# One ring of single PSUM banks, rounding scratch in PSUM, later block stores and a re-dealt set of sums, in a retention block followed by a SwiGLU feed-forward

## The chip, the cores and the metric

The kernel runs on one core of a Trainium2 chip. The metric is the device time of one execution in microseconds (us). The profile is that of one execution, taken by the hardware profiler. Its engine names are PE (TensorE, the matmuls; PEld is its weight load), DVE (VectorE), ACT (ScalarE), POOL (GpSimd) and SP (SyncE, which here only issues transfers). Lines such as L653 are lines of the kernel before.

## The reference

The weight matrices are fp64 arrays, the rest fp32. First a retention layer, then a normalised gated feed-forward on its output:

```python
# q, k, v: (8 batches, 8 heads, 576 positions, 64)
scores = scale * np.matmul(q, k.transpose(0, 1, 3, 2))
gamma = 1.0 - 2.0 ** (-5.0 - np.arange(H))
Dmat = np.where(rel >= 0, gamma ** rel, 0.0)      # rel = i - j
attn = np.matmul(scores * Dmat, v)
# (B,H,S,D) -> x: (4608 tokens, 512)
xn = x / np.sqrt(np.mean(x * x, -1) + 1e-6) * rms_g
g = xn @ w_gate                                    # 512 -> 1536
out = (g / (1 + np.exp(-g)) * (xn @ w_val)) @ w_out   # 1536 -> 512
```

The weight matrices are read as pairs of 32-bit words, a low and a high one.

## The kernel before

**Units.** The 4608 tokens are nine units of 512 (`u` 0 to 8). Attention for one batch and two heads is a *slot* (`j`, 32 of them): `scores`, `states`, `weigh`, `sums`, `values`, `carried`. A unit's feed-forward has two halves: *up* (gate and value, with the gating, into `h`) and *across* (`h` times `w_out`). Units 0 and 1 use plain matmuls for up (`up_plain`); units 2 to 8 use a scheme of seven products in place of eight for each 2 x 2 split (`up`), and every across uses that scheme twice, so seven products `xzwyxzw`, each made of seven smaller ones.

**Rounding.** While units 0 and 1 go up, the fp64 weights are turned to fp32 by integer work. There are 36 *halves* (512 KB loads, four scratch places `spare`, half `i` in place `i % 4`). A half takes three steps of the generator `rounding`: `exponent` (L862, VectorE, followed by two ScalarE instructions), `mantissa` (L877, L880, L884) and `join` (L901). The exponents lie in the last third of the scratch place. After every fourth half GpSimd makes the sums of the seven-product scheme (L912) and SP stores the block to DRAM: two transfers for an up block (`finish_set`, L922), seven for an out block (`finish_slice`, L928). Only then is the load of half `i + 4` issued (L849). Blocks come in the order up 0, 1, 2, out 0, up 3, out 1, up 4, 5, out 2. The loop over `up_plain` counts its 48 groups of matmuls in `now`; each group is one bank, four matmuls of 128 x 512, and then up to three rounding steps (`weights(3)`), so one half. Attention slots, the transposes of q and k (`prepare`) and their transfers (`fetch`) are hung on certain values of `now`.

**Across.** For every one of the seven products, four sums of quarters of its operand are needed (`inner_sums`, L694, four instructions of 128 x 384). They lie in one of two places of `inner`. In units 2 to 8 GpSimd makes all but four of the early ones (the list at L697 names units 0 and 1 only); sums 0 and 1 before the first product, sum `n + 2` after product `n`. The first half of a product (`late=False`) does without the sums. ScalarE keeps x, VectorE adds y, z and w to the kept values (`add`, L749). In the middle of it VectorE also normalises the next unit's x: `root_2`, then `norm_2` with four scalings (L514) and four sums of x (L524), all at step 6 of across.

**PSUM.** Eight banks. Three are one tile `trio` (scores and states of a slot; x and half of y in across); five rotate under one tag.

**Order.** The order of instructions on each engine is written by hand: the generators are driven by the loops in `start` and at the end, and each engine takes its instructions in that order. SP issues transfers in that order too.

Of the kernel before, what the change touches and what calls it, by code (L numbers as in the profile page):

```python
# [14 lines left out]
P = 128  # L15
# [26 lines left out]
def kernel(  # L42
# [234 lines left out]
    def scores(j):  # L277

        d = st[j]
        s = d["s"] = trio.tile([P, 3, 512], F32, tag="s", name=f"s_{j}")  # L280
        for c in range(NC + 1):
            i, odd = divmod(c, 2)
            c = min(c, NC - 1)
            for e in range(2):
                nc.tensor.matmul(
                    s[side(odd), e, i * L : i * L + L], lhsT=d["kT"][side(e), c * L : c * L + L],
                    rhs=d["qT"][side(e), c * L : c * L + L], start=True, stop=True,
                )

    def state_of(d, c):  # L290

        i, odd = divmod(c, 2)
        if odd and SC + i * L == 512:
            return d["last"][:, :L]
        return d["s"][:, 1, SC + i * L : SC + i * L + L] if odd else d["s"][:, 2, i * L : i * L + L]

    def states(j):

# [11 lines left out]
    def weigh(j):  # L310

        d = st[j]
        hp = jobs[j][1]
        s = d["s"]
        n = NFULL + 1
        ret = d["ret"] = att.tile([P, 2, n, L], F32, tag="ret", name=f"ret_{j}", bufs=1)
        for e in range(2):
            nc.vector.scalar_tensor_tensor(
                out=ret[:, e], in0=s[:, e, : n * L].rearrange("p (c k) -> p c k", k=L),
                scalar=float(_gamma(H)[2 * hp + e] ** -L),  # L320
                in1=causal.unsqueeze(1).to_broadcast([P, n, L]), op0=ALU.mult, op1=ALU.mult,
            )
# [177 lines left out]
        t_of[u] = y  # L500

    def norm_2(u):

        x = x_of[u]
# [6 lines left out]
        for c in range(NHP):  # L513
            nc.vector.scalar_tensor_tensor(  # L514
                out=x[:, c], in0=x[:, c], scalar=g[:, c : c + 1], in1=rb,
                op0=ALU.mult, op1=ALU.mult,
            )
        if u < 2:
            return
# [158 lines left out]
        return {A11: b11, S1: t1, S3: b12, S2: b11, A12: b21, S4: b22, A22: t1}  # L678

    def inner_of(u, n):  # L680
        return [inner[:, (7 * u + n) % 2, i] for i in range(4)]

    def inner_sums(u, n):

        x = operands_of(u)[ORDER[n]]
        x11, x12 = x[:, :NK, :P], x[:, :NK, P:]
        x21, x22 = x[:, NK:, :P], x[:, NK:, P:]
        i1, i3, i2, i4 = inner_of(u, n)
        eng = nc.vector if 7 * u + n in (4, 7, 10, 12) else nc.gpsimd
        for o, a, b, op in (  # L690
            (i1, x12, x11, ALU.subtract), (i3, x22, x12, ALU.subtract),
            (i2, i3, x11, ALU.add), (i4, x21, i2, ALU.subtract),
        ):
            eng.tensor_tensor(out=o, in0=a, in1=b, op=op)  # L694

    def across(u):
# [4 lines left out]
        b21, b22 = hh[:, NH:, :HU], hh[:, NH:, HU:]  # L701
        t1 = t1_of(u)
        operands = operands_of(u)
        tri = []
        vector = {}
        first = set()

        def banks_of(nm):

            if not tri:  # L710
                tri.append(trio.tile([P, 3, 512], F32, tag="s", name=f"s_out_{u}"))
            t = tri[0]
            if nm == "x":
                return t[:, 0], t[:, 1]
            if nm == "y":
                return t[:, 2], bank(f"yo_{u}")
            return bank(f"{nm}o_{u}"), bank(f"{nm}p_{u}")

        def product(n, nm, w, late):
# [30 lines left out]

        last = u == NU - 1
        if u > 1:
            inner_sums(u, 0)
            inner_sums(u, 1)
        yield
        for n, nm in enumerate("xzwyxzw"):
            w = piece("out", u, n)
            product(n, nm, w, False)
            yield
            product(n, nm, w, True)  # L760
            used()
            if n == 0:
                keep(3, "x")
                nc.vector.tensor_tensor(out=b11, in0=b12, in1=b11, op=ALU.add)
            elif n == 1:
                nc.vector.tensor_tensor(out=t1, in0=b21, in1=b11, op=ALU.subtract)
            elif n == 3:
                add(1, 3, "y")
                add(3, 1, "z")
                add(3, 3, "w")  # L770
                if last:
                    combine(3)
            elif n == 4:
                keep(0, "x")
                if last:
                    combine(0)
            elif n == 5:
                add(2, 1, "z")
                if last:
                    combine(2)  # L780
            elif n == 6:
                add(1, 1, "w")
                if last:
                    combine(1)
            if n + 2 < 7 or u == 0:
                inner_sums(u + (n + 2) // 7, (n + 2) % 7)
            yield
        if not last:
# [41 lines left out]
    def words_of(i):  # L830
        return spare[i % 4][:, :WORDS].bitcast(U32)

    def exp_of(i):
        return spare[i % 4][:, WORDS:]

    def load_half(i, queue):
        if i >= len(halves):
# [20 lines left out]

    def exponent(i):

        w, e = words_of(i), exp_of(i).bitcast(U32)
        nc.vector.tensor_scalar(  # L862
            out=e, in0=w[:, 1::2], scalar1=20, scalar2=0x7FF,
            op0=ALU.logical_shift_right, op1=ALU.bitwise_and,
        )
        f = exp_of(i)
        acts.extend((i, x) for x in (
            dict(out=f, in_=e, bias=most, scale=-1.0),
            dict(out=e, in_=f, bias=top, scale=-(2.0**23)),
        ))  # L870

    def mantissa(i):
# [7 lines left out]
        nc.vector.tensor_scalar(  # L880
            out=hi, in0=hi, scalar1=0xFFFFF, scalar2=0x100000,
            op0=ALU.bitwise_and, op1=ALU.bitwise_or,
        )
        nc.vector.scalar_tensor_tensor(  # L884
            out=lo.bitcast(F32), in0=lo, scalar=2.0**-32, in1=hi, op0=ALU.mult, op1=ALU.add
        )

    def join(i):
# [25 lines left out]
    def finish_set(k):  # L914
# [6 lines left out]
        for o, t in ((w_up_d[k][:, : 3 * BLOCK], w[:, :3]), (w_up_d[k][:, 3 * BLOCK :], s)):  # L921
            nc.sync.dma_start(out=o, in_=t.rearrange("p b c f -> p (b c f)"))  # L922

    def finish_slice(k):
        combine_blocks([slices[:, i, :4] for i in range(7)], S1)
        combine_blocks([slices[:, :, i] for i in range(7)], S1)
        for o in ORDER:
            nc.sync.dma_start(out=w_out_d[o][:, :, k], in_=slices[:, o])  # L928

    n_joined = 0  # L930
    due = False
    sets_used = [0] * 2 * NG
# [7 lines left out]
    def rounding():  # L940
# [4 lines left out]
        for i in range(len(halves)):  # L945
# [31 lines left out]

    def start():

        tables = list(zip((causal, gv, gc, gq, gx), (_causal_table(), *_decay_tables(H, D))))  # L980

        def table(i, queue):
# [51 lines left out]
            act(1)  # L1034
        gather(*squares.pop())
        fetch(FIRST)

        now = 0
        for u, k in (
            (0, 0), (1, 0), (0, 1), (1, 1), (0, 2), (1, 2), (0, 3), (1, 3), (0, 4), (0, 5), (1, 4),  # L1040
# [3 lines left out]
            for i, _ in enumerate(up_plain(u, k)):  # L1044
# [10 lines left out]
                    prepare(FIRST + (now - 10) // 6)  # L1055
                elif now in (12, 18):
                    fetch(FIRST + 1 + (now - 12) // 6)
                elif now == 36:
                    slot(FIRST, rest=False)
                elif now in (40, 42, 44):  # L1060
                    slot(FIRST + (now - 38) // 2)
                elif now in (41, 43, 45):
                    prepare(FIRST + (now - 37) // 2)
                    fetch(FIRST + (now - 35) // 2)
                elif now == 46:
# [25 lines left out]
        for i, _ in enumerate(across(1)):  # L1091
# [5 lines left out]
                root_2(2)  # L1097
            elif i == 8:
                norm_2(2)

    with tc.manual_schedule():
        start()
        for u in range(2, NU):
# [53 lines left out]
```

## Time and profile before

Two timed runs: 1238.75 and 1232.72 us, median 1235.74. The profiled execution spans 1230.5 us.

| stage of the profile | from, us | what it is |
|---|---|---|
| slots 0 to 7 | 0 | attention of batches 0 and 1, first halves rounded |
| up of units 0 and 1, rounding | 58 | 48 groups, slots 8 to 11 towards the end |
| across of units 0 and 1 | 305 | 14 products |
| units 2 to 6 | 376 | each up, four slots, across; about 125 us each |
| units 7 and 8 | about 1005 | up and across without slots |
| last sums and stores | 1224 | end |

Busy over the whole span: PE 1124.3 us, DVE 827.9, POOL 445.1, ACT 249.0. The profile's page also cuts the span in 40 equal slices of 30.8 us and gives each engine's busy share in tenths; `PEclk` is the granted TensorE clock in the same way. In a group line "x16 | 19.5, 1216" is the count, the busy time in us and the mean in ns; in a timeline line the first number is the start, the second the time, and the bracket the idle time before it and what ended it. Transfers move 249.22 MB, 203 GB/s in the mean.

### The profile page before, as it was taken

Reading aid. Unit: us, or ns where it says so; the run is one execution under the profiler, and the core shown is the slowest. Engines: PE = TensorE matmul, PEld = TensorE weight load, DVE = VectorE, ACT = ScalarE, POOL = GpSimd, SP = SyncE. Lnnn points to the kernel's source line nnn. Section 1 sums busy time; section 2 is a strip of 40 time slices with the busy share of each in tenths; the row PEclk is TensorE's granted clock in tenths of the full one; section 3 lists DMA queues with packets and bytes.
Section 4 is the critical chain, followed back from the end, with each engine's and each line's share of the span. In section 5 each row is a group of like instructions: output and inputs, shape, how many; then the busy total and the mean of one; then the engine's idle time right before and its main releaser. Section 6 shows DMA issues by size and latency. Waiting matters only on the chain. (4 is left out here: it accounts for less than half of the span.)

```text
span 1230.5 us, 24167 instructions
## 1 busy us (share of the span) xinstructions
PE 1124.3 (91%) x10086; PEld 925.9 (75%) x10086; DVE 827.9 (67%) x1398; ACT 249.0 (20%) x501; POOL 445.1 (36%) x356
## 2 busy tenths in 40 slices
PE   8889574898999998999899989999999999989997
PEld 6634231355989887988798888888888888879897
DVE  5899675857796779376937793779376834592555
ACT  5433132221111220112012201221122101201110
POOL 0033433342783018400850076006700670184036
PEclk9999887999999999999999999999999999999999
DMA  8566686538977885579557874787666546356361
GB/s 209 149 183 229 157 221 181 212 100 200 350 269 273 230 231 206 183 174 248 198 214 183 215 280 169 199 211 256 233 147 207 192 180 240 138 210 214 122 251 37
DMA packets 255421, 249.22 MB, mean 203 GB/s; under 512 B 193104, under 2 KB 232656, under 8 KB 241104
## 3 DMA queue, kind: packets, MB, share of 16 engines
q1 hardware_dynamic: 253456, 246.59, 64.4%
q8 instruction: 79, 1.29, 0.4%
q10 hardware_dynamic: 1856, 1.09, 0.3%
q14 instruction: 30, 0.25, 0.1%
HBM read 217.55 MB, written 30.08 MB: 201 GB/s over the span
## 5 line engine op out<-in xcount | busy, mean ns | idle before, releaser
L694 POOL TENSOR_TENSOR vi<-h 128x384 f32<-128x384 f32 x78 | 106.2, 1377 | 482.4 <-DVE h L605 459.9
L647 PE MATMUL up<-x,ring 128*128 128x512 f32 x384 | 180.7, 628 | 46.1 <-DVE ring L653 20.6
L647 PEld LDWEIGHTS up<-x,ring 128*128 128x128 f32 x384 | 75.4, 201 | 145.3 <-issue 83.7
L586 PE MATMUL x<-x,ring 128*128 128x256 f32 x672 | 161.4, 383 | 0.0
L586 PE MATMUL w<-sums,ring 128*128 128x256 f32 x672 | 158.7, 379 | 0.0
L586 PE MATMUL z<-x,ring 128*128 128x256 f32 x672 | 158.7, 379 | 0.0
L586 PEld LDWEIGHTS z<-x,ring 128*128 128x128 f32 x672 | 127.7, 190 | 19.9 <-issue 2.9
L586 PEld LDWEIGHTS w<-sums,ring 128*128 128x128 f32 x672 | 127.7, 190 | 17.4
L586 PEld LDWEIGHTS x<-x,ring 128*128 128x128 f32 x672 | 125.1, 190 | 17.4
L800 POOL TENSOR_TENSOR vi<-vi 128x512 f32<-128x512 f32 (+1 forms) x56 | 67.1, 1210 | 42.5 <-DVE vi L749 40.0
L586 PE MATMUL y<-sums,ring 128*128 128x256 f32 x336 | 79.6, 379 | 1.7 <-issue 1.7
L586 PEld LDWEIGHTS y<-sums,ring 128*128 128x128 f32 x336 | 63.8, 190 | 10.7 <-issue 2.1
L731 PE MATMUL s_out<-ring,vi 128*128 128x128 f32 x540 | 67.5, 278 | 2.8 <-POOL vi L694 2.8
L593 DVE TENSOR_TENSOR h<-u,w 128x512 f32<-128x512 f32 x42 | 28.9, 687 | 60.9 <-PE w L586 44.0
L745 ACT COPY vi<-s_out 128x512 f32<-128x512 f32 (+1 forms) x36 | 17.4, 535 | 250.0 <-PE s_out L731 224.7
L731 PEld LDWEIGHTS s_out<-ring,vi 128*128 128x128 f32 x540 | 64.1, 194 | 4.4 <-POOL vi L694 3.9
L912 POOL TENSOR_TENSOR ring<-ring 128x512 f32<-128x512 f32 x24 | 34.5, 1436 | 86.5 <-DVE ring L901 85.6
L612 ACT COPY m<-x 128x512 f32<-128x512 f32 x42 | 24.6, 585 | 189.4 <-PE x L586 189.4
L593 DVE TENSOR_TENSOR u<-m,y 128x512 f32<-128x512 f32 x42 | 28.8, 685 | 50.0 <-PE y L586 47.9
L731 PE MATMUL s_out<-ring,h 128*128 128x128 f32 x384 | 51.8, 292 | 11.3 <-DVE vi L749 11.3
L731 PEld LDWEIGHTS s_out<-ring,h 128*128 128x128 f32 x384 | 49.4, 206 | 13.7 <-DVE vi L749 12.8
L334 DVE SCALAR_TENSOR_TENSOR sum<-sum,gc,s 128x64 f32<-128x64 f32 x192 | 53.9, 281 | 6.8
(214 smaller groups left out, 1930.1 us busy)
## 6 DMA issues: line engine op xcount, KB each, us to landing
ring<-w_out_blocks SPq DMA_DIRECT2D x63, 1344.0 KB, 6.6
ring<-w_up_blocks SPq DMA_DIRECT2D x42, 1792.0 KB, 7.6
w_out_blocks<-vi SPq DMA_DIRECT2D x21, 448.0 KB, 5.7
out_dram<-vi SPq DMA_DIRECT2D x64, 128.0 KB, 3.0
qraw<-in_q_dram SPq DMA_DIRECT2D x96, 72.0 KB, 5.3
kraw<-in_k_dram SPq DMA_DIRECT2D x96, 72.0 KB, 3.2
k<-in_k_dram SPq DMA_DIRECT2D x48, 128.0 KB, 2.9
v<-in_v_dram SPq DMA_DIRECT2D x48, 128.0 KB, 2.8
```

What stands on the lines that cost most here:

```text
L334: nc.vector.scalar_tensor_tensor(out=t[:, c], in0=t[:, c - 1], scalar=gc[:, hp : hp + 1], in1=part, op0=ALU.mult, op1=ALU.add,)
L586: nc.tensor.matmul(ps[:, i * HU : i * HU + HU], lhsT=w[:, PLACE[blk], c, i * P : i * P + P], rhs=t_of[u][blk][:, c], start=(start and i == ...
L593: nc.vector.tensor_tensor(out=o, in0=a, in1=pairs_of(ps), op=ALU.add)
L612: nc.scalar.copy(out=s1, in_=pairs_of(x_))
L647: nc.tensor.matmul(ps, lhsT=w[:, PLACE[blk], c % 2, i * P : i * P + P], rhs=x_of[u][:, c], start=(c == 0), stop=(c == NHP - 1),)
L694: eng.tensor_tensor(out=o, in0=a, in1=b, op=op)
L731: nc.tensor.matmul(ps, lhsT=lhs[:, c], rhs=w[:, s, c], start=((nm, s // 4) not in first), stop=False, skip_group_check=True,)
L745: nc.scalar.copy(out=o, in_=ps)
L800: eng.tensor_tensor(out=t[:, :, o], in0=t[:, :, x], in1=t[:, :, y], op=ALU.add)
L912: nc.gpsimd.tensor_tensor(out=t[o], in0=t[x], in1=t[y], op=op)
```

## The change

It has five parts.

1. **Single banks.** `trio` goes; all eight banks rotate under one tag. A slot's scores and states are three tiles, and each of x, y, z, w in across takes two.
2. **Rounding in PSUM.** From the up stage on, a half's exponents lie in a bank `exp_i`, and L880 writes its masked high words to a bank `man_i` in place of the scratch place. So each of the five VectorE instructions has at most one operand in SBUF that it reads. In groups 0 to 3 one rounding step follows a group instead of three.
3. **Stores behind loads.** `finish_set` and `finish_slice` put their stores on a list; they are issued two halves (up) or four halves (out) after the block's last join, ahead of that half's load. The last out block's stores go after the up pieces of unit 0.
4. **Sums of across, units 2 to 8.** Sum 1 goes to VectorE, ahead of the `b11` addition; sum 2 gets a third place, in `sums_x`; three sums are made before the first product, 3, 4, 5, 6 after products 0, 1, 3, 4.
5. **Norm spread out.** The scalings of the next x come one each at steps 3 to 6 of across, the sums of x at step 8, behind the additions. Slots and transposes in the up stage move by a group or two (the first slot from 36 to 34).

```diff
-    trio = ctx.enter_context(tc.tile_pool(name="trio", bufs=1, space=PS))
-    banks = ctx.enter_context(tc.tile_pool(name="banks", bufs=5, space=PS))
+    banks = ctx.enter_context(tc.tile_pool(name="banks", bufs=8, space=PS))
...
-        s = d["s"] = trio.tile([P, 3, 512], F32, tag="s", name=f"s_{j}")
+        s = d["s"] = [bank(f"s_{j}_{i}") for i in range(3)]
...
     def inner_of(u, n):
-        return [inner[:, (7 * u + n) % 2, i] for i in range(4)]
+        if u > 1 and n == 2:
+            t = sums_x.rearrange("p i c t -> p (i c t)")
+            return list(t.rearrange("p (i c t) -> i p c t", i=4, c=NK))
+        at = (0, 1, None, 0, 1, 0, 1)[n] if u > 1 else (7 * u + n) % 2
+        return [inner[:, at, i] for i in range(4)]
...
-        eng = nc.vector if 7 * u + n in (4, 7, 10, 12) else nc.gpsimd
+        eng = nc.vector if (n == 1 if u > 1 else 7 * u + n in (4, 7, 10, 12)) else nc.gpsimd
...
         if u > 1:
-            inner_sums(u, 0)
-            inner_sums(u, 1)
+            for n in range(3):
+                inner_sums(u, n)
...
-            if n + 2 < 7 or u == 0:
+            if u > 1:
+                if n in (0, 1, 3, 4):
+                    inner_sums(u, {0: 3, 1: 4, 3: 5, 4: 6}[n])
+            elif n + 2 < 7 or u == 0:
...
+        exps[i] = bank(f"exp_{i}") if in_psum else spare[i % 4][:, WORDS:]
...
+        m = bank(f"man_{i}").bitcast(U32) if in_psum else hi
         nc.vector.tensor_scalar(
-            out=hi, in0=hi, scalar1=0xFFFFF, scalar2=0x100000,
+            out=m, in0=hi, scalar1=0xFFFFF, scalar2=0x100000,
...
-            out=lo.bitcast(F32), in0=lo, scalar=2.0**-32, in1=hi, op0=ALU.mult, op1=ALU.add
+            out=lo.bitcast(F32), in0=lo, scalar=2.0**-32, in1=m, op0=ALU.mult, op1=ALU.add
...
+        stores.append((n_joined + 3, [
+            (o, t.rearrange("p b c f -> p (b c f)"))
...
+        stores.append((n_joined + 5, [(w_out_d[o][:, :, k], slices[:, o]) for o in ORDER]))
...
             join(i)
+            n_joined += 1
+            store_blocks(n_joined)
             load_half(i + 4, nc.sync)
-            n_joined += 1
...
-                elif now == 36:
+                elif now == 34:
                     slot(FIRST, rest=False)
...
-                weights(3)
+                weights(3 if now > 3 else 1)
...
             if (u, k) == (0, 5):
                 weights_to(len(halves))
+                store_blocks(len(halves) + 9)
                 refill(1)
...
                 if i == 2:
                     root_2(u + 1)
-                elif i == 6:
-                    norm_2(u + 1)
+                elif i in (3, 4, 5, 6):
+                    scale_x(u + 1, (i - 3,))
+                elif i == 8:
+                    sums_of_x(u + 1)
```

More of the change, by code (lines that the diff above doesn't have):

```diff
@@ L285, in scores @@
                 nc.tensor.matmul(
-                    s[side(odd), e, i * L : i * L + L], lhsT=d["kT"][side(e), c * L : c * L + L],
+                    s[e][side(odd), i * L : i * L + L], lhsT=d["kT"][side(e), c * L : c * L + L],
                     rhs=d["qT"][side(e), c * L : c * L + L], start=True, stop=True,
@@ L294, in state_of @@
             return d["last"][:, :L]
-        return d["s"][:, 1, SC + i * L : SC + i * L + L] if odd else d["s"][:, 2, i * L : i * L + L]
+        return d["s"][1][:, SC + i * L : SC + i * L + L] if odd else d["s"][2][:, i * L : i * L + L]
     def states(j):
@@ L318, in weigh @@
             nc.vector.scalar_tensor_tensor(
-                out=ret[:, e], in0=s[:, e, : n * L].rearrange("p (c k) -> p c k", k=L),
+                out=ret[:, e], in0=s[e][:, : n * L].rearrange("p (c k) -> p c k", k=L),
                 scalar=float(_gamma(H)[2 * hp + e] ** -L),
@@ L502, in norm_2, with scale_x @@
     def norm_2(u):
+        scale_x(u, range(NHP))
+    def scale_x(u, chunks):
         x = x_of[u]
@@ L512, in norm_2 @@
             nc.tensor.matmul(rb, lhsT=ones, rhs=t_of[u], start=True, stop=True)
-        for c in range(NHP):
+        for c in chunks:
             nc.vector.scalar_tensor_tensor(
@@ L517, in norm_2, with sums_of_x @@
             )
-        if u < 2:
-            return
+    def sums_of_x(u):
+        x = x_of[u]
         b11, b12 = x[:, :2, :HU], x[:, :2, HU:]
@@ L703, in across @@
         operands = operands_of(u)
-        tri = []
         vector = {}
@@ L708, in banks_of @@
         def banks_of(nm):
[L710 to L716, printed above, removed]
             return bank(f"{nm}o_{u}"), bank(f"{nm}p_{u}")
@@ L831, in words_of @@
         return spare[i % 4][:, :WORDS].bitcast(U32)
+    exps = {}
     def exp_of(i):
-        return spare[i % 4][:, WORDS:]
+        return exps[i]
     def load_half(i, queue):
@@ L920, in finish_set @@
         )
-        for o, t in ((w_up_d[k][:, : 3 * BLOCK], w[:, :3]), (w_up_d[k][:, 3 * BLOCK :], s)):
-            nc.sync.dma_start(out=o, in_=t.rearrange("p b c f -> p (b c f)"))
+        stores.append((n_joined + 3, [
+            (o, t.rearrange("p b c f -> p (b c f)"))
+            for o, t in ((w_up_d[k][:, : 3 * BLOCK], w[:, :3]), (w_up_d[k][:, 3 * BLOCK :], s))
+        ]))
     def finish_slice(k):
@@ L926, in finish_slice, with store_blocks @@
         combine_blocks([slices[:, :, i] for i in range(7)], S1)
-        for o in ORDER:
-            nc.sync.dma_start(out=w_out_d[o][:, :, k], in_=slices[:, o])
+        stores.append((n_joined + 5, [(w_out_d[o][:, :, k], slices[:, o]) for o in ORDER]))
+    def store_blocks(n):
+        while stores and stores[0][0] <= n:
+            for o, t in stores.pop(0)[1]:
+                nc.sync.dma_start(out=o, in_=t)
+    stores = []
+    in_psum = False
     n_joined = 0
@@ L978, in start @@
     def start():
+        nonlocal in_psum
         tables = list(zip((causal, gv, gc, gq, gx), (_causal_table(), *_decay_tables(H, D))))
@@ L1036, in start @@
         fetch(FIRST)
+        in_psum = True
         now = 0
@@ L1057, in start @@
                     fetch(FIRST + 1 + (now - 12) // 6)
-                elif now == 36:
+                elif now == 34:
                     slot(FIRST, rest=False)
[L1060 to L1065, printed above, removed]
+                elif now in (40, 42, 45):
+                    slot(FIRST + {40: 1, 42: 2, 45: 3}[now])
+                elif now in (41, 44, 46):
+                    n = {41: 2, 44: 3, 46: 4}[now]
+                    prepare(FIRST + n)
+                    fetch(FIRST + n + 1)
+                elif now == 47:
                     close(FIRST + NHP - 1)
-                weights(3)
+                weights(3 if now > 3 else 1)
                 act(2)
@@ L1099, in start @@
                 norm_2(2)
+                sums_of_x(2)
     with tc.manual_schedule():
```

## The prediction

> **What bounds the kernel now.** I read the page first: share of each engine, then the slices.
>
> ```profile
> PE 1124.3 (91%) x10086; PEld 925.9 (75%) x10086; DVE 827.9 (67%) x1398; ACT 249.0 (20%) x501; POOL 445.1 (36%) x356
> ...
> PE   8889574898999998999899989999999999989997
> POOL 0033433342783018400850076006700670184036
> PEclk9999887999999999999999999999999999999999
> ```
>
> TensorE is the bound nearly everywhere, so only its gaps can be won: the dip in slices 5 to 9 (a slice is 30.8 us), and one lighter slice every fourth, where POOL peaks. The clock row drops in the same places. The chain of waits covers only the last 8 us (VectorE's closing sums), so I went on with PE's own waits and then with the timeline of each engine around them.
>
> **Gap 1, weight rounding (58 to 252 us).** Groups of up_plain (one bank, eight records each; 48 of them, numbered by `now`) run at 7.11/2 = 3.56 us when nothing waits: the first line below is groups 4 to 18 without a gap. Then PE, POOL, SP and VectorE at the longest hole:
>
> ```profile
> 82.33 53.24 PE L647 MATMUL up<-x,ring 128*128 128x512 f32 x120 [3.81 <-DVE x L514]
> 157.42 12.04 PE L647 MATMUL up<-x,ring 128*128 128x512 f32 x24 [16.40 <-DVE ring L653]
> 127.03 14.08 POOL L912 TENSOR_TENSOR vi<-vi 128x512 f32<-128x512 f32 x7 [6.20 <-DVE vi L901]
> 141.13 8.47 SPq L928 DMA_DIRECT2D w_out_blocks<-vi  x7
> 149.66 1.52 SPq L849 DMA_DIRECT2D sums<-in_moe_w_val_dram  x1
> 156.34 0.43 DVE L862 TENSOR_SCALAR sums<-sums 128x512 uint32<-128x512 uint32 x1 [13.50 <-DMA sums<-in_moe_w_val_dram]
> ```
>
> SP issues in order: the stores of out block 0 wait for POOL's sums (until 141.1), the next load stands behind them, VectorE starves 13.5 us, PE 16.4. Out block 1 does the same at 198 to 210 (VectorE 11.8, PE 8.8). The groups of VectorE by shape show the second cost:
>
> ```profile
> L884 DVE SCALAR_TENSOR_TENSOR ring<-ring 128x512 f32<-128x512 uint32 x16 | 19.5, 1216 | 0.6
> L884 DVE SCALAR_TENSOR_TENSOR t<-t 128x512 f32<-128x512 uint32 x8 | 5.6, 694 | 0.3
> L880 DVE TENSOR_SCALAR ring<-ring 128x512 uint32<-128x512 uint32 x16 | 17.0, 1063 | 0.6
> L880 DVE TENSOR_SCALAR t<-t 128x512 uint32<-128x512 uint32 x8 | 3.4, 428 | 0.3
> L653 DVE TENSOR_TENSOR ring<-ring,up 128x512 f32<-128x512 f32 x10 | 6.8, 678 | 0.0
> ```
>
> The same instruction takes 694 ns (on t), or on average 1216 (on ring): single ones are 0.69 or 1.64 us, the latter while POOL runs; L653, with one operand in PSUM, keeps 678 beside POOL.
>
> **Gap 2, across.** A product of seven (42 pairs of records) takes 4.69 us, so an across could take 32.8. Unit 2's runs from 462.9 to about 503.9, 41.0 us; units 3 to 6 the same, unit 7 39.4, unit 8 33.9. PE in unit 2, then VectorE:
>
> ```profile
> 471.94 0.94 PE L731 MATMUL zp<-ring,vi 128*128 128x128 f32 x6 [0.83 <-POOL vi L694]
> 488.18 3.85 PE L731 MATMUL s_out<-ring,h 128*128 128x128 f32 x18 [1.61 <-DVE vi L749]
> 476.23 5.69 DVE L514 SCALAR_TENSOR_TENSOR x<-x,rms_k,sq 128x512 f32<-128x512 f32 x4
> 487.45 0.67 DVE L749 TENSOR_TENSOR vi<-vi,s_out 128x512 f32<-128x512 f32 x1
> ```
>
> POOL's sums are late: it makes four instructions for each of the seven, only two sums ahead, and they take 1.32 to 1.44 us, 1.00 when VectorE is quiet. VectorE's norm ops take 1.42 instead of 0.69 in turn, so its y addition starts at 487.45; and the fifth product (x again) waits for that addition only because x and y share the three-bank tile. The wait costs 1.6 us and a slow clock (18 records in 3.85, not 2.17).
>
> **What the Trainium skill says.** "SBUF — State Buffer", section "Who interferes with whom": VectorE and GpSimd share a port pair as an exclusive lock; a VectorE instruction with two SBUF inputs, or in a two-port mode, contends with GpSimd, one with a single SBUF input outside those modes does not. The rows above agree (678 always; 694 against 1640). "VectorE: DVE Perf Modes", section "Why PSUM operands drop a tier", and Mode 2×_2P: the doubled fp32 rate of a one-source op needs SBUF on both sides. So L862 and L880 (420 to 430 ns) lose it when they write PSUM; no row here shows one, so I bound it: below by 430, above by 750; I take 680, the one-rate L653. "TensorE: Matmul & The Clock Gate", section "What's actually happening": an idle window of some 3.4 us halves the clock; the 5.90 us that one group takes after the gap at 192 us agrees.
>
> **The change, part by part.**
>
> *Rounding in PSUM.* Start-to-start, undisturbed, a half costs VectorE now 0.34+0.72+0.46+0.73+0.61 = 2.86 us (L862, 877, 880, 884, 901). With exp and man in PSUM the two one-source ops rise to about 0.60 and 0.72, L877 no longer has to finish first (0.60): 3.26. That is +0.4 x 32 halves = 13 us, against what the lock costs now: L884 16 x 0.52, L877 16 x 0.51 + 9 x 0.27, L880 16 x 0.63, L901 10 x 0.35, L862 3: 36 us. Net VectorE gain 23.
>
> *Stores behind loads.* Stores of an up block go two halves after its last, of an out block four later (14.4 us at 3.6, POOL needs 13.9). The starving of 13.5 and 11.8 goes, but not wholly: when out stores are issued they hold SP 8.5 us and the next load lands about 15 us after (141.1 to 156.3), while VectorE needs it two steps later, 7.2 us: a stall of 7.5, twice. A transfer of q and k (9.5 us of SP, 123.8 to 133.2) stands right before out block 0's stores: another 4; the one before it: 2. Together 21 us (none to 40).
>
> *Sum of groups 4 to 35.* VectorE: 32 x 3.26 = 104, 16 multiplications x 0.6 = 10, two transposes of pairs 3, split joins 12 x 0.15 = 2, the attention slot moved to 34 with 4: 123; plus stalls 21 = 144. PE at full pace: 32 x 3.56 + 2 = 116, so VectorE bounds. Banks tie the two: exp, man and up rotate through eight, three a step, so PE may lead by about two steps; a stall of VectorE reaches PE. One rounding step instead of three in groups 0 to 3 lets the norm come sooner: group 4 starts at 77.6 instead of 82.3 (rb at 76, L514 at 77, since the multiplication then waits only for PE). VectorE from 79.6: group 36 starts at about 79.6 + 144 - 3.5 = 220, now 247.4: **27 us**.
>
> *Groups 36 to 47.* Now 57.9 us to the first across (305.3). Then 12 x 3.56 + 3 slots x 2.3 + close 1.3 = 51, and I leave 3 us of waits for q and k (now 3.7, with a slow clock): **4 us**.
>
> *Single banks.* Across 0 and 1 lose the waits for y, 0.78 and 1.33 with 0.1 each: **2.3**. In attention slots and up pieces the tile eight places back has always been read by then (z of a piece waits for av of the slot before, as now): nothing.
>
> *One sum of seven on VectorE, third place.* From across start: POOL finishes sum 0 at -1.2, VectorE the last difference at 5.6. Then sum 1 (VectorE) and sum 2 (POOL, in sums_x, free since the last product of up at 0) alternate under the lock at 1.4 a pair: both done by 10.4. Product 1 ends at 11.1 (now 11.2); product 2 finds its sums ready, 15.8 (now 17.9). Queued behind VectorE's four: L764, which sum 3 needs (12.1); POOL does sum 3 by 17.4, PE's late half of product 3 starts 17.8: 20.5 (now 23.6 plus the wait). Sum 4 by 24.2, product 4 ends 25.2. The additions come after the four scalings, 23.5 to 26.9; product 5 needs z read, 25.4: no loss. Products 5 and 6 end at 30.1 and 34.8. So 6.2 us saved in units 2 to 6, 4.6 in unit 7, none in 8 (no norm, so no lock now): **35.6 us**. Splitting the scaling over four steps and the sums of x later cost nothing: the next unit's first S2 product starts 1.7 us after it begins, and the last sum of x ends near 32.
>
> Sum 27 + 4 + 2.3 + 35.6 = 69; from the median 1235.7: **1167 us**.
>
> **Rivals.**
> *A, transfers bound the rounding.* Needed there: 32 loads of 0.52 MB, five up blocks of 1.8, two out blocks of 3.1, two transfers of 1.1: 34 MB in 140 us, 243 GB/s; the out stores at 145 to 155 ran at 263 to 287 GB/s with the DMA engines all busy. For: stores and loads now compete in the same two steps. Against: 82 to 135 us ran at full pace with 211 GB/s. Stalls of 40 leave 8: total 50, 1186.
> *B, VectorE bounds the across.* It gets four more ops under the lock, ahead of L764; if they go last each time, sums 3 and z come 4 us late and only 2 a unit remain: 12 instead of 36: 1191. A and B together: 1211.
> *C, slower.* One ring of banks makes PE wait for VectorE where it led by five groups, PSUM ops are slower than 680, and slots wait for banks: +16 in rounding (two ops x 0.26 x 30), 32 slots x 0.5: about 1268. Against it: L653 and the additions (0.54 to 0.67) show no PSUM penalty.
> *D, no stall at all* in rounding: 1146.
>
> **Numbers.** Forecast 0.52, A 0.17, B 0.14, A and B 0.06, C 0.04, D 0.07. Range 1142 to 1204: leaves out C, A with B, and part of D. Faster by over 2% (below 1211): 0.90; within 2%: 0.06; slower: 0.04.
>
> **What would show it.** L884 and its like near 690 whatever POOL does, L862 and L880 near 680; PE's holes of 16.4 and 8.8 gone, with two waits of 5 to 8 us behind out stores; group 36 near 220; across at 34 to 36 us with the first L694 wait in product 1 and no wait of the second x for VectorE. Wrong if PE waits for man or exp banks in each step, if one-source ops to PSUM cost over 0.8, or if across stays near 40.

## The result

The changed kernel takes 1158.77 us (two runs, 1158.69 and 1158.85), the kernel before 1235.74: a ratio of 0.938, 95% interval 0.928 to 0.948. Run again beside three of the experiments (3, 4 and 5) it took 1160.15 us, ratio 0.941 (0.938 to 0.943). The profiled execution spans 1157.1 us instead of 1230.5 (the medians lie 77 us apart, the two profiles 73). L numbers below are those of the changed kernel: the exponent is L867, the mantissa's three instructions are L882, L886 and L890, join is L907, a group's matmul and gating product are L650 and L656, GpSimd's block sums L918, stores L941, loads L853; in across, matmuls are L730, the sums of quarters L701, the additions L748, scalings L515, sums of x L527.

The page of the changed kernel, the lines that answer to those of before (slices are now 28.9 us):

```profile
PE 1105.9 (96%) x10086; PEld 918.7 (79%) x10086; DVE 822.3 (71%) x1426; ACT 247.5 (21%) x501; POOL 401.0 (35%) x328
...
PE   8899877998999999999999999999999999999997
...
POOL 0023623534752018301730164006500660174035
PEclk8999989998999999999999999999999999999999
```

TensorE works as long as before within 2%, in a span 6% shorter; the dip 5, 7, 4 in slices 5 to 7 is now 8, 7, 7, and the lighter slice in each unit is gone. Where the time came from, read from the starts of the matmul groups in the timeline:

| from, to | before, us | after, us | saved | predicted |
|---|---|---|---|---|
| start to group 4 | 82.3 | 76.8 | 5.5 | 4.7 |
| group 4 to 36 | 165.2 | 140.2 | 25.0 | 22 |
| group 36 to the first across | 57.8 | 55.2 | 2.6 | 4 |
| first across to that of unit 2 | 157.6 | 155.9 | 1.7 | 2.3 |
| across of unit 2 to that of unit 8 | 727.3 | 689.7 | 37.6 | 35.6 |
| rest | 40.3 | 39.3 | 1.0 | 0 |

When group 36 starts depends also on how far TensorE runs ahead of VectorE (run 6 below). The end of the rounding's last join doesn't: 252.3 us before, 219.9 after.

**Rounding.** VectorE's groups by shape, from 60 to 300 us (count, then busy us and mean ns):

```profile
L890 DVE SCALAR_TENSOR_TENSOR ring<-ring,man 128x512 f32<-128x512 uint32 x16 | 11.0, 689 | 0.6
...
L890 DVE SCALAR_TENSOR_TENSOR t<-t,man 128x512 f32<-128x512 uint32 x8 | 5.5, 689 | 0.3
...
L886 DVE TENSOR_SCALAR man<-ring 128x512 uint32<-128x512 uint32 x16 | 11.0, 686 | 0.0
...
L886 DVE TENSOR_SCALAR man<-t 128x512 uint32<-128x512 uint32 x8 | 5.5, 687 | 0.0
...
L656 DVE TENSOR_TENSOR ring<-ring,up 128x512 f32<-128x512 f32 x12 | 8.1, 675 | 0.0
```

With the second operand in PSUM the instruction that took 1216 ns on the ring takes 689, as on `t`, where it ran while GpSimd was idle. L886 paid for it (428 ns on `t` before, 687 now), and so did L867 (437 on `sums` before, 689 now). The timeline around the former holes, TensorE first, then GpSimd, SP and VectorE:

```profile
135.61 13.04 PE L650 MATMUL up<-x,ring 128*128 128x512 f32 x30
153.83 6.75 PE L650 MATMUL up<-x,ring 128*128 128x512 f32 x8 [5.18 <-DVE vi L907]
163.17 29.56 PE L650 MATMUL up<-x,ring 128*128 128x512 f32 x64 [2.59 <-DVE vi L907]
199.32 1.22 PE L650 MATMUL up<-x,ring 128*128 128x512 f32 x1 [6.59 <-DVE ring L656]
...
124.89 12.65 POOL L918 TENSOR_TENSOR vi<-vi 128x512 f32<-128x512 f32 x7 [7.87 <-DVE vi L907]
...
143.35 9.26 SPq L941 DMA_DIRECT2D w_out_blocks<-vi  x7
152.71 1.41 SPq L853 DMA_DIRECT2D sums<-in_moe_w_out_dram  x1
...
148.76 0.42 DVE L907 SCALAR_TENSOR_TENSOR vi<-ring,exp 128x256 f32<-128x256 f32 x1 [5.29 <-DMA w_out_blocks<-vi]
...
159.72 0.69 DVE L867 TENSOR_SCALAR exp<-sums 128x512 uint32<-128x512 uint32 x1 [5.95 <-DMA sums<-in_moe_w_out_dram]
...
196.06 0.69 DVE L867 TENSOR_SCALAR exp<-sums 128x512 uint32<-128x512 uint32 x1 [6.49 <-DMA sums<-in_moe_w_val_dram]
```

The holes of 16.4 and 8.8 us became 5.2, 2.6 and 6.6. GpSimd's sums are done at 137.5, and the stores don't wait for them any more; but they still hold SP from 143.4 to 152.6, and the load behind them lands at 159.7, where VectorE has waited 5.95 us. One wait is new: the first join of out block 1 overwrites `slices` and has to wait 5.29 us until the stores have read them.

**Across.** Unit 2, which starts at 428.13; TensorE, then VectorE:

```profile
436.86 0.94 PE L730 MATMUL zp<-ring,vi 128*128 128x128 f32 x6 [0.34 <-DVE vi L701]
438.13 0.94 PE L730 MATMUL zo<-ring,vi 128*128 128x128 f32 x6 [0.34 <-DVE vi L701]
...
448.28 1.50 PE L730 MATMUL xo<-ring,h 128*128 128x128 f32 x12
...
452.97 1.50 PE L730 MATMUL zo<-ring,h 128*128 128x128 f32 x12
...
449.76 0.68 DVE L748 TENSOR_TENSOR vi<-vi,yo 128x512 f32<-128x512 f32 x1
...
452.95 1.30 DVE L527 TENSOR_TENSOR sums<-x 128x512 f32<-128x512 f32 x1
```

Only the second product (z) waits for sums, twice 0.34 us. The second x starts at 448.28, before VectorE adds y at 449.76. Each of units 2 to 7 takes 34.4 us.

### The profile page after: what moved, and what is told of

Its sections match the earlier page's. It is cut to its first block, busy times and chain, and to the rows that moved or that the text cites. A ratio compares the mean times of both kernels' runs of the same rounds, so it can differ in the third digit from the quotient of the medians.

```text
span 1157.1 us, 24137 instructions
## 1 busy us (share of the span) xinstructions
PE 1105.9 (96%) x10086; PEld 918.7 (79%) x10086; DVE 822.3 (71%) x1426; ACT 247.5 (21%) x501; POOL 401.0 (35%) x328
## 5 line engine op out<-in xcount | busy, mean ns | idle before, releaser
L701 POOL TENSOR_TENSOR vi<-h 128x384 f32<-128x384 f32 x64 | 78.2, 1237 | 502.1 <-DVE h L608 456.8
L650 PE MATMUL up<-x,ring 128*128 128x512 f32 x384 | 176.2, 617 | 20.4 <-DVE ring L656 8.2
L650 PEld LDWEIGHTS up<-x,ring 128*128 128x128 f32 x384 | 74.1, 197 | 117.2 <-issue 82.7
L802 POOL TENSOR_TENSOR vi<-vi 128x512 f32<-128x512 f32 (+1 forms) x56 | 67.2, 1211 | 22.3 <-DVE vi L748 19.8
L596 DVE TENSOR_TENSOR h<-u,w 128x512 f32<-128x512 f32 x42 | 28.9, 688 | 61.0 <-PE w L589 46.8
L610 ACT ACTIVATE h<-h 128x512 f32<-128x512 f32 x63 | 39.5, 629 | 80.3 <-DVE h L596 80.3
L918 POOL TENSOR_TENSOR vi<-vi 128x512 f32<-128x512 f32 (+1 forms) x24 | 40.3, 1680 | 44.2 <-DVE vi L907 19.5
L744 ACT COPY vi<-xo 128x512 f32<-128x512 f32 x18 | 10.6, 586 | 210.4 <-PE xo L730 178.4
L596 DVE TENSOR_TENSOR u<-u,z 128x512 f32<-128x512 f32 x42 | 28.9, 688 | 26.7 <-PE z L589 25.7
L701 POOL TENSOR_TENSOR vi<-h,vi 128x384 f32<-128x384 f32 x32 | 46.2, 1445 | 2.5
L918 POOL TENSOR_TENSOR ring<-ring 128x512 f32<-128x512 f32 x24 | 30.5, 1276 | 47.0 <-DMA w_up_blocks<-ring 15.8
```

Source lines behind the costliest of these rows:

```text
L596: nc.vector.tensor_tensor(out=o, in0=a, in1=pairs_of(ps), op=ALU.add)
L610: nc.scalar.activation(out=o, in_=c, func=AF.Silu)
L650: nc.tensor.matmul(ps, lhsT=w[:, PLACE[blk], c % 2, i * P : i * P + P], rhs=x_of[u][:, c], start=(c == 0), stop=(c == NHP - 1),)
L744: nc.scalar.copy(out=o, in_=ps)
L802: eng.tensor_tensor(out=t[:, :, o], in0=t[:, :, x], in1=t[:, :, y], op=ALU.add)
L918: nc.gpsimd.tensor_tensor(out=t[o], in0=t[x], in1=t[y], op=op)
```

## The experiments

Each kernel ran four times beside runs of the kernel before. "Behind" is the changed kernel's place for the stores, "in front" that of the kernel before.

| kernel | us, median (range) | ratio to before (95%) |
|---|---|---|
| changed, again | 1160.15 (1159.0–1161.6) | 0.941 (0.938–0.943) |
| 1 scratch in SBUF | 1177.92 (1175.6–1178.4) | 0.954 (0.952–0.956) |
| 2 stores in front | 1198.32 (1195.5–1199.4) | 0.971 (0.968–0.973) |
| 3 norm in one piece | 1197.46 (1194.0–1201.8) | 0.971 (0.967–0.974) |
| 4 sum 1 on GpSimd | 1174.23 (1172.6–1176.4) | 0.952 (0.949–0.954) |
| 5 two places | 1157.23 (1156.5–1160.9) | 0.939 (0.936–0.941) |
| 6 single banks alone | 1213.03 (1212.4–1214.0) | 0.983 (0.981–0.986) |
| 7 spread stores | 1150.44 (1149.0–1152.3) | 0.932 (0.930–0.935) |
| 8 refill first | 1151.05 (1147.7–1152.4) | 0.933 (0.929–0.936) |
| 9 end of the up stage alone | 1161.16 (1158.2–1161.6) | 0.941 (0.938–0.944) |
| 10 q and k behind across 0 | 1150.64 (1145.8–1152.4) | 0.931 (0.928–0.934) |
| 11 half blocks | 1143.41 (1142.4–1147.4) | 0.926 (0.925–0.928) |

**The changed kernel again**, as the base. 

> The changed kernel itself, beside the other three on the same chip, as their base: 1155 to 1162 us in either theory.

### Rounding: scratch in PSUM and stores behind loads

```diff
# 1, scratch in SBUF
-        in_psum = True
+        in_psum = False
# 2, stores in front
-        stores.append((n_joined + 3, [
+        stores.append((n_joined, [
-        stores.append((n_joined + 5, [(w_out_d[o][:, :, k], slices[:, o]) for o in ORDER]))
+        stores.append((n_joined, [(w_out_d[o][:, :, k], slices[:, o]) for o in ORDER]))
```

**1.** 

> The changed kernel with exponents and mantissas back in SBUF, all else kept. Port-lock theory: groups 4 to 35 cost VectorE some 36 us of waiting for GpSimd again and save 13 us of doubled rate; a part hides in the waits for loads (23 us now), so the stage grows by 12 to 20 us: 1171 to 1179 us. Rival, the order of the stores alone made the gain in rounding and the lock lies beside it: 1156 to 1162 us.

18 us slower than the changed kernel. VectorE in 60 to 300 us by shape, and SP and VectorE at the end of the up stage:

```profile
L890 DVE SCALAR_TENSOR_TENSOR ring<-ring 128x512 f32<-128x512 uint32 x16 | 19.3, 1208 | 0.6
...
L886 DVE TENSOR_SCALAR ring<-ring 128x512 uint32<-128x512 uint32 x16 | 15.1, 947 | 0.6
```

```profile
253.20 8.85 SPq L941 DMA_DIRECT2D w_out_blocks<-vi  x7
...
263.84 4.14 SPq L159 DMA_DIRECT2D qraw<-in_q_dram  x4
...
273.43 0.78 DVE L256 STREAM_TRANSPOSE qT<-qraw 128x576 f32<-128x576 f32 x1 [7.20 <-DMA qraw<-in_q_dram]
```

The long instructions are back, although VectorE waits less for loads (18.9 us from 76 to 260, 23.3 in the changed kernel). The rounding ends later, the last out block's stores go at 253.20 instead of 232.58, and the transfer of q and k behind them makes VectorE's transposes wait 7.20 us, and with them a slot on TensorE (9.61 us).

**2.** 

> The changed kernel with each block's stores issued at once, ahead of the next load, as before. Queue theory: after each of out blocks 0 and 1 VectorE waits for 12.7 us of GpSimd sums and some 15 us of stores and load, less two or three steps of 3.3: about 19 us each, where it now waits 12 and 6.5; an up block costs 1 to 2 us more: 1176 to 1188 us. Rival, the faster rounding in PSUM alone made the gain: 1156 to 1163 us.

38 us slower, more than the theory said. GpSimd, SP, VectorE and TensorE at out block 0:

```profile
133.43 12.64 POOL L918 TENSOR_TENSOR vi<-vi 128x512 f32<-128x512 f32 x7 [14.27 <-DVE vi L907]
...
146.10 8.49 SPq L941 DMA_DIRECT2D w_out_blocks<-vi  x7
154.64 1.51 SPq L853 DMA_DIRECT2D sums<-in_moe_w_val_dram  x1
...
161.62 0.69 DVE L867 TENSOR_SCALAR exp<-sums 128x512 uint32<-128x512 uint32 x1 [20.59 <-DMA sums<-in_moe_w_val_dram]
...
165.00 5.41 PE L650 MATMUL up<-x,ring 128*128 128x512 f32 x8 [20.09 <-DVE ring L907]
```

The chain is the one of before (last join, GpSimd's sums, seven stores, one load). VectorE comes to its wait at 141.0 (142.8 before), but the load lands at 161.6 (156.3): 20.59 us where it waited 13.5. Run 1, run 2, the changed kernel and the kernel before make a square; "waits" is what VectorE waits for transfers from 76 to 260 us:

| first across starts at (waits), us | stores in front | stores behind |
|---|---|---|
| scratch in SBUF | 305.3 (38.0) | 291.1 (18.9) |
| scratch in PSUM | 310.4 (62.7) | 272.3 (23.3) |

PSUM alone brings nothing: what VectorE gains it waits longer, 62.7 instead of 38.0 us. Later stores alone bring 14. Both bring 33: with the loads in time VectorE bounds, and only then its speed counts. The ends of the last join say the same (252.3 and 240.4 us in the upper row, 259.6 and 219.9 in the lower). One cell is not quite like the others: the kernel before (305.3) also has the three-bank tile, three rounding steps in groups 0 to 3 and its slots at their old places. Run 6, which has single banks, starts its first across at 305.1; the other two differences weren't run by themselves. So the 38 us of the stores with PSUM and the 19 us of PSUM with late stores are shown; the 14 and the loss of 5 may have a part of those two in them.

### Across: banks, sums, norm, third place

```diff
# 3, norm in one piece
-                elif i in (3, 4, 5, 6):
-                    scale_x(u + 1, (i - 3,))
-                elif i == 8:
+                elif i == 6:
+                    norm_2(u + 1)
                     sums_of_x(u + 1)
# 4, sum 1 on GpSimd
-        eng = nc.vector if (n == 1 if u > 1 else 7 * u + n in (4, 7, 10, 12)) else nc.gpsimd
+        eng = nc.vector if u < 2 and 7 * u + n in (4, 7, 10, 12) else nc.gpsimd
# 5, two places
-        at = (0, 1, None, 0, 1, 0, 1)[n] if u > 1 else (7 * u + n) % 2
+        at = n % 2 if u > 1 else (7 * u + n) % 2
...
-                if n in (0, 1, 3, 4):
-                    inner_sums(u, {0: 3, 1: 4, 3: 5, 4: 6}[n])
+                if n + 2 < 7:
+                    inner_sums(u, n + 2)
# 6, single banks alone: the kernel before, with part 1 of the change
```

**6.** 

> The kernel before with single banks only. Theory of the false wait: the waits of the second x for the y addition (12.6 us of PE over nine across) and the slow clock after them (about 1.6 us in units 2 to 6) go: 1216 to 1222 us. Rival, the wait only moves to GpSimd's sums or to the z additions right after: 1229 to 1238 us.

20.5 us faster than before (1233.5 beside it), a little more than the theory said, and nearly all of it in across (18 of the 20 us between the two profiles): units 2 to 7 take 38.0 us each (before 41.2 in units 2, 3 and 6 and 39.6 in 4, 5 and 7, 40.4 in the mean), unit 8 33.0 (34.1), the two of units 0 and 1 68.5 (71.2). The rounding gains nothing: the first across starts at 305.1. With eight banks in place of five TensorE does run further ahead and starts group 36 at 230.5 (247.5 before), but VectorE's last join ends at 250.3 (252.3), and TensorE gives its lead back in waits of 5.62, 3.54 and 4.64 us at the slots and a slow clock after them. In unit 2 (from 458.9) the second x no longer waits 1.61 us for VectorE; what is left are waits for GpSimd's sums, such as

```profile
467.90 0.94 PE L722 MATMUL zp<-ring,vi 128*128 128x128 f32 x6 [0.83 <-POOL vi L693]
...
475.98 0.94 PE L722 MATMUL wo<-ring,vi 128*128 128x128 f32 x6 [0.47 <-POOL vi L693]
...
481.59 0.94 PE L722 MATMUL yo<-ring,vi 128*128 128x128 f32 x6 [0.47 <-POOL vi L693]
```

**3.** 

> The changed kernel with the four scalings and the four sums of the next x together at step 6 of across, ahead of the additions, as before. Order theory: the four sums (5.6 us under the lock) stand ahead of the z addition that product 5 needs, so product 5 waits about 4 us in units 2 to 7: 1176 to 1186 us. Rival, only the re-dealt sums matter: 1156 to 1163 us.

37 us slower, more than expected: 40.3 to 41.6 us for each across of units 2 to 7. Unit 2, from 430.8, TensorE and then VectorE:

```profile
459.83 2.93 PE L730 MATMUL zo<-ring,h 128*128 128x128 f32 x12 [4.03 <-DVE vi L748]
...
446.81 5.70 DVE L515 SCALAR_TENSOR_TENSOR x<-x,rms_k,sq 128x512 f32<-128x512 f32 x4
452.64 1.27 DVE L527 TENSOR_TENSOR sums<-x 128x512 f32<-128x512 f32 x1
...
458.04 0.67 DVE L748 TENSOR_TENSOR vi<-vi,yo 128x512 f32<-128x512 f32 x1
...
459.10 0.67 DVE L748 TENSOR_TENSOR vi<-vi,zo 128x512 f32<-128x512 f32 x1
```

Four scalings and four sums of x, 11.2 us in one piece, stand ahead of the additions. In the changed kernel the scalings are ahead of them too, but the four sums (5.4 us there) come behind. So y comes at 458.04 (in the changed kernel 21.6 us after the start of across, here 27.2), z at 459.10, and the second z waits 4.03 us for it in each of six units (24.2 us in all). After the wait 12 records take 2.93 us instead of 1.50.

**4.** 

> The changed kernel with sum 1 of units 2 to 8 on GpSimd again, three places kept. Rate theory: seven sums of about 5.2 us under the lock do not fit beside an across of 32.8, PE waits 3 to 5 us more in each of units 2 to 7: 1176 to 1190 us. Rival, the third place (GpSimd further ahead) made the gain: 1157 to 1166 us.

14 us slower, a little less than the theory said: 37.1 us for each across of units 2 to 7, where GpSimd now makes all seven sums, as it does in the kernel before. Unit 2, from 424.7:

```profile
433.74 0.94 PE L730 MATMUL zp<-ring,vi 128*128 128x128 f32 x6 [0.83 <-POOL vi L701]
435.13 0.94 PE L730 MATMUL zo<-ring,vi 128*128 128x128 f32 x6 [0.47 <-POOL vi L701]
...
440.41 0.94 PE L730 MATMUL wp<-ring,sums 128*128 128x128 f32 x6 [0.99 <-POOL sums L701]
441.81 0.94 PE L730 MATMUL wo<-ring,sums 128*128 128x128 f32 x6 [0.47 <-POOL sums L701]
```

Four waits for GpSimd, 2.76 us, where the changed kernel has twice 0.34 for VectorE. Runs 3, 4 and 6 together (6 lacks the third place, shown next to be worth nothing):

| across of units 2 to 7, single banks, us each | norm in one piece | norm spread out |
|---|---|---|
| sum 1 on GpSimd | 38.0 | 37.1 |
| sum 1 on VectorE | 41.0 | 34.4 |

Sum 1 on VectorE costs 3 us with the norm ahead of the additions, and saves 2.7 with the sums of x behind them.

**5.** 

> The changed kernel with two places for the sums, sum n+2 made after product n, sum 1 still on VectorE. Theory: sum 2 can't get past its first instruction before the last difference at 5.6 us after the start of across, and place 0 is free at 4.7, so the third place is worth 0 to 1 us a unit: 1157 to 1165 us. Rival, the place is what lets GpSimd keep up: 3 us a unit, 1175 us or more.

No difference to the changed kernel: across again 34.4 us. The third place isn't needed; two places and the old order `n + 2` after product `n` do as well.

### What is left: from the last out stores to unit 2

**7.** Each out block's seven stores in four lots behind four loads, the second transfer of q and k moved from group 18 to 32, and slot 11 closed before the last transposes instead of after them.

```diff
-        stores.append((n_joined + 5, [(w_out_d[o][:, :, k], slices[:, o]) for o in ORDER]))
+        for n, at in enumerate(((A11, S1), (A12, A22), (S3, S2), (S4,))):
+            stores.append((n_joined + 4 + n, [(w_out_d[o][:, :, k], slices[:, o]) for o in at]))
...
-                elif now in (12, 18):
-                    fetch(FIRST + 1 + (now - 12) // 6)
+                elif now in (12, 32):
+                    fetch(FIRST + (1 if now == 12 else 2))
...
-                elif now in (41, 44, 46):
-                    n = {41: 2, 44: 3, 46: 4}[now]
+                elif now in (41, 44, 47):
+                    n = {41: 2, 44: 3, 47: 4}[now]
...
-                elif now == 47:
+                elif now == 46:
```

> The changed kernel with an out block's seven stores in groups of two behind four successive loads, in the order in which the next out block overwrites them, the transfer of q and k at group 18 moved to 32, and the last close of the up stage before the last prepare instead of after. Queue theory: VectorE's waits for loads and stores in groups 4 to 35 (23 us) fall to 6 or less and PE's 4.4 us wait ahead of across 0, with its slow clock, goes: 1136 to 1144 us. Rival, the DMA engines are full there and the waits only move: 1150 to 1158 us.

The theory fails in its time, which is in the rival's range. Group 36 starts at 206.1, 11 us earlier, VectorE waits 13.5 us for transfers instead of 23.3 (6 were expected), and the first across starts at 257.5, 14.8 earlier. But across of units 0 and 1 takes 76.9 us instead of 70.4: TensorE waits for the third out block it reads back, and comes back slowly (12 records in 2.90 us instead of 1.50):

```profile
272.89 2.90 PE L730 MATMUL wo<-ring,h 128*128 128x128 f32 x12 [5.87 <-DMA ring<-w_out_blocks]
```

So 6.5 of the 14.8 us are gone.

**8, 9 and 10** look for that wait in SP's order: the last transfer of q and k stood ahead of that block. In 8 (built on 7) it goes behind the refill, 9 is the same edit of the up stage's end with the changed kernel's stores, in 10 (on 7) it goes into the across of unit 1.

```diff
                     prepare(FIRST + n)
-                    fetch(FIRST + n + 1)
+                    if n < 4:
+                        fetch(FIRST + n + 1)
...
# 8 and 9
         refill()
+        fetch(FIRST + 5)
# 10, in across(1)
+            elif i == 2:
+                fetch(FIRST + 5)
```

> The kernel with spread stores, and the last transfer of q and k of the up stage issued behind the refill of out blocks instead of ahead of it. Theory (the order in SP's queue made the 5.9 us wait for the third out block): with q and k out of the way the block is issued about 7 us earlier (near 259 instead of 266.3), the across of units 0 and 1 takes 68.5 us as in the kernel with single banks alone, instead of 76.9, and the time is 1140 to 1144 us. Rival (the block's place and the transfer itself bind: the last up product ends at 257.5, the block takes 6 to 7 us): a wait of 2 to 5 us with a slow clock stays, 1146 to 1150 us.

> The changed kernel with its stores as they are; only the end of the up stage is edited: slot 11 is closed before the last transposes of q and k instead of behind them, and the last transfer of q and k goes behind the refill. Theory: PE's 4.4 us wait for ScalarE's copy before the first across goes, and with it the slow clock of its first two groups of records (2.93 and 1.35 us instead of 1.50 and 0.83): 6.4 us less than the changed kernel, 1151 to 1154 us. Rival (something else ends as late, such as the third out block or the gating products): 1157 to 1161 us.

> As the kernel with spread stores, but the last transfer of q and k of the up stage is issued in the across of unit 1, behind the refills of all the out blocks of unit 0 (its slot comes 40 us later). Theory (the wait for an out block moves to the first block behind that transfer, wherever it stands: third block with the transfer ahead of the refill, fourth with it right behind): now no block is behind it, the wait of 5.5 to 5.9 us and the slow clock after it go, the across of units 0 and 1 takes 68.5 us instead of 76.9: 1140 to 1144 us. Rival (out blocks stream at the rate at which their places come free, and the wait would show later whatever the order): the across of units 0 and 1 takes 74 to 77 us, 1147 to 1152 us.

All three miss their theory, and are near or in the range of their rival. The 4.44 us wait before across goes in 9, but nothing is won: the wait for an out block comes at the fourth block (5.1 us), as in 8 (5.5); in 10 it comes at the thirteenth (4.0), and the first across starts 4 us later than in 7. From the first store of the last out block to unit 2's up the kernels take 109.9 (changed), 112.6 (7), 112.0 (8), 111.6 (9) and 110.0 us (10), and move 30.2 MB in each, in packets that take 85 to 87% of the DMA engines' time. That pointed to the amount instead of the order.

**11.** 8 with half of each out block left out of the transfer for units 0 and 1.

```diff
-            nc.sync.dma_start(out=ring[:, a:z], in_=src)
+            m = z - (OUT // 2 if kind == "out" and u < 2 else 0)
+            nc.sync.dma_start(out=ring[:, a:m], in_=src[:, : m - a])
```

> The kernel with spread stores and the refill first, but of every out block that the across of units 0 and 1 loads, only the first half is transferred (672 of 1344 KB, 14 blocks; the rest of the place keeps what lay there, so the output of these two units is not the reference's). Instructions and their order are the same. Theory (from the last out stores to the up of unit 2 the transfers bind: 30.2 MB in 110 to 112 us in every order tried): with 9.4 MB less the wait of 5.5 us for an out block and the slow clock behind it go, and some of the waits of q and k before it; the across of units 0 and 1 takes 68.5 us, and the time is 1139 to 1144 us. Rival (the times at which places come free, or the order of issue, bind, not the amount): the across stays at 74 to 77 us, 1147 to 1152 us.

The same stretch of 8, its transfers (packets, MB, share of the 16 engines) and its wait; then those of 11:

```profile
q1 hardware_dynamic: 31782, 30.04, 86.5%
```

```profile
278.26 2.90 PE L730 MATMUL yo<-ring,h 128*128 128x128 f32 x12 [5.50 <-DMA ring<-w_out_blocks]
```

```profile
q1 hardware_dynamic: 31779, 20.36, 69.5%
```

```profile
276.51 1.58 PE L731 MATMUL yo<-ring,h 128*128 128x128 f32 x12 [0.57 <-DMA ring<-w_out_blocks]
```

With a third of the bytes gone, in as many packets, the wait shrinks to 0.57 us, across of units 0 and 1 takes 69.3 us instead of 76.9, the stretch 104.3 instead of 112.0. So in 8 the bytes to transfer set that stretch, and not the order in which SP issues them or the number of packets; for 7, 9 and 10, with as many bytes in 110 to 113 us, the same is likely. Whether it is the sum of all bytes or the time of a single block isn't separated: a block lands 5.1 us after its issue in the median, where it took 7.2 in 8. 11 leaves out half of what units 0 and 1 need and is no version to use.

**The best version** that computes everything is 7, with 8 and 10 beside it: 1150.4 us, ratio 0.932 (0.930 to 0.935) against 0.941 (0.938 to 0.943) for the changed kernel, about 0.9% less.

## Why the prediction was right, by its steps

The time comes from where the prediction has it, the rounding and the across, and most of the waits that it names go. That the sums come so near is in part luck: some terms stand in the wrong place, and errors cancel.

**Rounding in PSUM.** Right in size: L867, L882, L886 and L890 take 685 to 690 ns (680 taken), a half 3.25 us (3.26). "Net VectorE gain 23" holds only together with the later stores; the square shows that alone it is worth nothing. The prediction added the two parts in one sum and so didn't show this.

**Stores behind loads.** Stalls of 21 us predicted, 23.3 measured. Behind the stores of out block 0 the prediction has 7.5 us and 4 more for the q and k ahead of them; measured are 12.0, but half of that is a wait that it doesn't have, that of a join for `slices` to be stored (5.29 + 0.80), and the load came only 5.95 us after. That the two sums agree is luck. Behind those of out block 1 it has 7.5, measured are 6.49; the rest are small waits for loads, 4.8 us (2 predicted). Group 36 starts at 217.1 instead of the 220 forecast, since groups 4 to 36 took 140.2 us where the sum gave 142.4.

**Groups 36 to 47.** 4 predicted, 2.6 measured: the wait allowed for q and k was 3 us, it was 4.44 (TensorE waits for ScalarE, which waits for v), and a slow clock followed (12 records of the first across in 2.93 us instead of 1.50).

**Single banks.** "2.3" for units 0 and 1: run 6 measures 2.7, in the changed kernel the slow clock leaves 0.8 of it. The term was mis-sized in another way: single banks are worth 20.5 us by themselves. The prediction saw the wait of the second x and its cause, the shared tile, but put its 2.4 us in the mean of units 2 to 7 under the sums, and the 1.1 of unit 8 at "none".

**One sum on VectorE, third place.** "35.6" for units 2 to 8, measured 37.6, of it 36.2 in the across themselves. Split by the runs: 6 x 2.4 = 14 from single banks, 6 x 3.6 = 22 from sum 1 and the spread norm together. The reading "41.0 us; units 3 to 6 the same" is wrong for units 4 and 5, which took 39.6: the saving is 6.8 us in units 2, 3 and 6 and 5.2 in 4, 5 and 7, not 6.2 in five and 4.6 in one. "Sum 2 ... in sums_x" was no part of it: run 5. "Splitting the scaling ... cost nothing" is true, but misses what it is for: without it, sum 1 on VectorE makes the across 3 us longer.

**Rivals.** A (transfers bound the rounding): no, the waits stay at 23 us; but transfers come to bind right behind it, once the rounding ends 11 us earlier still (runs 7 to 11). B (VectorE bounds the across): not as the kernel is, yes with the norm in one piece. C: PSUM operands took 0.69 us, no more; a slot waits for banks only in runs 1 and 6, where TensorE had run ahead of VectorE. D: stalls of 23 us remained; run 7 removes 10 of them.

## What to carry to other kernels

Ask of every saving which resource is the next to end last: here a faster VectorE was worth nothing until its loads came in time, and earlier loads were worth less than half until it was faster. When an engine's in-order queue gets more work, put what another engine waits for ahead of what nobody waits for yet; four sums of x ahead of six additions or behind them decided over 37 us. A wait that moves to another transfer whenever the order is changed may be a matter of the amount; transferring less shows it.

## What was not expected of the hardware

How long TensorE must stand still to come back slowly. The Trainium skill, "TensorE: Matmul & The Clock Gate", section "What's actually happening", has the clock at half after an idle window of about 3.4 us. Waits of 3.59, 4.03, 4.44 and 5.50 us (runs 4 and 3, the changed kernel, run 8) agree, with 12 records in 2.90 to 2.93 us after them instead of 1.50, and one of 1.72 us (run 1, 1.58 us after it). Others don't: after waits of 2.58 (run 5) and 2.08 us (run 2) 12 records took 2.56 and 2.90 us, in the kernel before a group took 5.40 us instead of 3.56 after a wait of 2.85 (at 186.9), and after 3.37 us in the up stage of the changed kernel (at 131.2) five groups ran at full pace. And in the kernel before, the second x waits 1.61 us in each of units 2 to 7, but the records after it are slow in units 2, 3 and 6 alone. Unit 2, whose line the prediction shows, took 3.85 us for 18 records; unit 4:

```profile
739.48 2.27 PE L731 MATMUL s_out<-ring,h 128*128 128x128 f32 x18 [1.61 <-DVE vi L749]
```

The measurements decide: the length of the last wait alone isn't what sets the clock here. What does stays open.

GpSimd gained too: its sums of out block 0 (seven instructions) took 14.08 us before, 13.71 in run 1 (scratch in SBUF), 12.65 in the changed kernel and 12.64 in run 2 (scratch in PSUM).
